# Loads in smaller pieces and a new order of the front in a spectral block with a gated feed-forward, one core

## The chip, the cores and the metric

The kernel runs on one core of one Trainium2 chip. The metric is the device time of one execution in microseconds (us). Before the change it is 486.74 us, the median of three runs (485.81 to 487.13). Five engines work side by side, each through its own queue in order: TensorE (PE, matmuls), VectorE (DVE), ScalarE (ACT), GpSimd (POOL) and SyncE (SP, which only issues DMA transfers here). They meet through semaphores.

## The reference

A is a spectral filter over one 2048 x 576 matrix, B a gated feed-forward part. Both are fed by a layer norm and added to their input. In bf16:

```python
def _A_ref(x, w_r, w_i):
    B, S, D = x.shape                       # 1, 2048, 576
    X = jnp.fft.rfft2(x.astype(jnp.float32), axes=(-2, -1))
    X = X * (w_r + 1j * w_i)                # 2048 x 289
    return jnp.fft.irfft2(X, s=(S, D), axes=(-2, -1)).astype(jnp.bfloat16)

def _B_ref(x, w_gate, w_up, w_down):        # 576 x 4608, 576 x 4608, 4608 x 576
    return (_gelu(x @ w_gate) * (x @ w_up)) @ w_down

h = x + _A_ref(_layernorm(x, axis=-1), A_w_r, A_w_i)
h2 = h + _B_ref(_layernorm(h, axis=-1), B_w_gate, B_w_up, B_w_down)
```

## The kernel before

The 2048 tokens lie in 16 tiles of 128 (tile c holds the tokens p * 16 + c). The Fourier transforms are matmuls with tables of cosines and sines that lie in device memory. The work has four parts:

- **The front** (0 to about 20 us): loads, the first layer norm, and the 128-point transforms over tokens within each tile.
- **Stages D, B, T, V, R** (to about 43 us): the transform over the 576 features (D), the 16-point transform (B, with the table BT), the product with the spectral weights (T), and the way back over 16 points (V and R, with the table VT).
- **The way back** over features and tiles (to about 55 us), with the first residual and the second layer norm.
- **The feed-forward part** (from 55 us), four blocks of 512 tokens, nearly all on TensorE.

The class `Prog` collects operations with the keys that they read and write. An operation waits for the last writer of what it reads, and for the writers and readers of what it overwrites. Each engine runs its operations in the order in which the program names them; so order is set by the order of calls, and for the front this is a string of tokens, `SEQ1`. The letter is the kind, the number the tile, the group or the output, and a last letter A, D or P names the engine:

- `B`, `b`: batch-norm statistics of one half of a tile on DVE (L496). `S`, `Q`: sum and sum of squares of a tile on ACT instead (L488, L492); `m`: square of the mean for such a tile on POOL (L499). The tiles with a `Q` are `ACT_TILES`.
- `v`: variances of a group of tiles on DVE (L505, L508). `q`: square root on ACT (L512). `c`: reciprocal on DVE (L517). The groups are tiles 0-1, 2-3, 4-6, 7-9, 10-12 and 13-15.
- `n`: the negated columns of a group's tiles on POOL (L569); `t`: copies of their tail columns on POOL (L574).
- `x`: the token table `ATB` scaled by the reciprocal deviations into `ATS` (L522 on POOL, one operation for a group; L527 on DVE, one for each tile).
- `M`: the 128-point transform of a group on TensorE (L553): five outputs in the order k = 1, 0, 3, 2, 4, each in a PSUM bank of its own. Two matmuls are needed for each tile and output, 20 for a group of two tiles and 30 for a group of three. Output n = 5 * group + place goes to bank (n + 1) mod 8.
- `k`: matmuls of zeros as fillers on TensorE (L538); the last two digits are how many.
- `E`: eviction of output n from PSUM into the tile `U` (L564). If there is an `F` with the same number, `E` takes only the first half (the frequencies that stage D takes first) and `F` the second.

`LORD` is the order of the loads of tokens (`x`, by tiles) and of the token table (`a`, by tiles), all issued by SP. Behind them SP issues the feature table FT, the first half of BT, the planes w_i and w_r of the spectral weights with VT between them, and at the end the second pieces of VT and BT. The weights are copied once more across the partitions (`dup_w`): on POOL (L732), on DVE (L730) and by DMAs from POOL's queue. The second of DVE's copies and of POOL's must be there before T2, the first of stage T.

`SEQF` is the order of the stages behind the front. It begins with D2 D0 d2 D1 d0 d1 B2 (a capital D is the first half of a product's matmuls, the small d the second half and the eviction, L642 and L608). Its banks are handed out in a fixed way: D2 writes banks 0 and 1, D0 2 and 3, D1 4 and 5, B2 6 and 7. Banks 0 and 1 held the outputs 23 and 24 of the front, so D2 waits until these are evicted. `ACT_TILES` also set how many operations compute the negative means at L747 on POOL, one for each run of tiles of a kind.

Of the kernel before, what the change touches and what calls it, by code (L numbers as in the profile page):

```python
# [20 lines left out]
NPRE = 8  # L21
PARTS = ((0, 256), (256, 512))
GROUPS = ((0, 2), (2, 4), (4, 7), (7, 10), (10, 13), (13, 16))
SEQ1 = """B0 b0 S3 B2 Q3 n0 B1 b1 b2 n1 t0 m3P t2 v0 v1 n2 t1 q0 c0 k14 x0D q1 M0 E0A S4 m4P c1 x1D n3 E2A k104 b5 t3 b7 Q4 E1A M1 E7A B5 B6 E8A b6 B7 v2 q2 B11 E5A B8 c2 x2P E3A E9A b8 b9 B9 v3 E6A n4 B12 Q13 E4A k206 M2 b10 q3 c3 b11 S13 x3P E11A B10 t4 b12 v4 E10A B14 m13P E14A M3 q4 c4 x4P E12A E13A t5 b14 E15A b15 B15 v5 E16A E18D E17A q5 M4 E20A E19A E23A c5 x5D n5 E24A F24D F23D E21A M5 E25A E26D E22A E28D E27A E29D F25A F29D F26A F27A F28A F22A""".split()
LORD = "x0-2 x2-4 a0-4 x4-8 a4-8 x8-12 x12-16 a8-16".split()
SPLIT = tuple(int(w[1:-1]) for w in SEQ1 if w[0] == "F")
ACT_TILES = tuple(int(w[1:]) for w in SEQ1 if w[0] == "Q")
SEQF = """D2 D0 d2 D1 d0 d1 B2 D5 B0 d5 T2 D3 B1 d3 D4 T0 T1 B5 d4 D8 B3 d8 D7 T3 B4 d7 V0 D6 v0 V1 T5 d6 v1 R0 V2 r0 v2 T4 B6 D9 B8 T6 V3 d9 D11 v3 d11 B7 D10 B9 d10 V6 V4 T7 v6 v4 V5 B10 v5 R1 D12 T8 r1 d12 B11 T9 V7 D14 v7 T10 d14 D13 B12 d13 D15 T11 V9 T12 d15 v9 V8 B13 v8 R2 r2 T13 B14 T14 B15 V12 V10 v12 v10 V13 V11 T15 v13 V14 v11 v14 V15 R3 v15 r3""".split()
# [9 lines left out]
def _np_bf16(a):  # L38
    npdt = mybir.dt.np(BF16)
    return np.ascontiguousarray(np.asarray(a, dtype=np.float32).astype(npdt))  # L40
# [291 lines left out]
def _build(nc, A_x, A_w_r, A_w_i, B_w_gate, B_w_up, B_w_down, out):  # L332
    P = Prog(nc)
    T = build_tables()
    dram = {n: nc.inline_tensor(_np_bf16(T[n]), name="c_" + n.lower()) for n in T}
    PE, DVE, ACT, SP, POOL = "pe", "dve", "act", "sp", "pool"
# [52 lines left out]
    BT = sb.alloc("BT", [128, 2, 2, 128], BF16)  # L389
    VT = sb.alloc("VT", [128, 6, 2, 128], BF16)  # L390
# [47 lines left out]
    def x_load(i, c0, c1):  # L438
        P.dma(SP, XO[:, c0:c1, 0:D], xv[:, c0:c1, :], f"x{i}", w=[("X", c) for c in range(c0, c1)])

    def atb_load(i, c0, c1):
        P.dma(SP, ATB[:, c0:c1, :], tabs[:, c0:c1, :], f"atb{i}", w=[("ATB", c) for c in range(c0, c1)])

    for i, w in enumerate(LORD):
        (x_load if w[0] == "x" else atb_load)(i, int(w[1:].split("-")[0]), int(w.split("-")[1]))
    P.dma(SP, FT[:, :, :].rearrange("p a b -> p (a b)"), dram["FTAB"][:, :], "ft", w=["FT"])
    P.dma(SP, BT[:, 0, :, :].rearrange("p b c -> p (b c)"), dram["BTAB"][:, 0:256], "bt", w=["BT"])

    def w_up(pl, hf):
        g0, g1 = ((0, 9), (9, 16))[hf]  # L450
# [5 lines left out]
    def w_down(pl, hf, sls=(0, 1, 2, 3), eng=SP, sem=""):  # L456
        g0, g1 = ((1, 9), (9, 16))[hf]
        src = (A_w_r, A_w_i)[pl].tensor
        for sl in sls:
            p0 = 64 * (sl // 2) + 32  # L460
            P.dma(eng, WS[p0 + sl % 2:p0 + 32:2, sl // 2, pl, g0:g1, :], bass.AP(src, (64 + 16 * (3 - sl) + 16 - g0) * K2, [[128 * K2, 16], [-K2, g1 - g0], [1, K2]]),
                  f"w{pl}{hf}{sem}", w=[("W", hf, pl, 2 + sl)])

    def w_zero(pl):
        for jp in range(2):
            P.dma(SP, WS[64 * jp + 32:64 * jp + 64, jp, pl, 0, :], bass.AP((A_w_r, A_w_i)[pl].tensor, (64 + 32 * jp) * K2, [[128 * K2, 16], [(-16 if jp else 48) * K2, 2], [1, K2]]),
                  f"wz{pl}", w=[("W", 2, pl, jp)])

    for pl in (1, 0):
        w_up(pl, 0)  # L470
        w_down(pl, 0)
    P.dma(SP, VT[:, 0, :, :].rearrange("p b c -> p (b c)"), dram["VTAB"][:, 0:256], "vt", w=["VT"])
    for pl in (1, 0):
        w_up(pl, 1)
        w_down(pl, 1, (0, 1, 2, 3) if pl else (0, 1))
    for pl in (1, 0):
        w_zero(pl)
    P.dma(SP, VT[:, 1, :, :].rearrange("p b c -> p (b c)"), dram["VTAB"][:, 256:512], "vt1", w=["VT1"])
    P.dma(SP, BT[:, 1, :, :].rearrange("p b c -> p (b c)"), dram["BTAB"][:, 256:512], "bt1", w=["BT1"])
    GORD = list(range(1, NG)) + [0]  # L480
    wkeys = [[("W", hf, pl, h) for pl in range(2) for h in range(6 if hf < 2 else 2)] for hf in range(3)]

# [99 lines left out]
    P.op(ACT, lambda a: a.activation(SA[:, 0, 0:1], EPT[:, 0:1], ACTF.Sqrt), r=["EPT"], w=[("SA0", 0)])  # L582
    for w in SEQ1:
        a = w[1:]
# [9 lines left out]
    for t, w in enumerate(SEQF):  # L594
        k, i = w[0], w[1:].rstrip("abc")
        if k in "DBVR":
            b = min((b for b in used if b not in busy), key=lambda b: used[b])
# [4 lines left out]
        elif k in "dvr":  # L602
            b = FB[k.upper(), int(i)]
# [137 lines left out]
    c = 0  # L741
    while c < NT:
        c1 = c + 1
# [5 lines left out]
        c = c1  # L749
# [34 lines left out]
    for w in SEQF:  # L784
        i = int(w[1:].rstrip("abc"))
# [26 lines left out]
    for t, w in enumerate(SEQ):  # L812
        k, i = w[0], int(w[1:].rstrip("ADSP"))
        if k in "INu":
            b = min((b for b in range(2 * ing, 4) if b not in held), key=lambda b: last[b])
# [3 lines left out]
        elif k in "ioUEae":  # L819
            b = SLOT[{"i": "I", "o": "N", "U": "u", "E": "I", "a": "N", "e": "u"}[k], i] // 2  # L820
# [145 lines left out]
    for w in SEQ:  # L966
        a = w[1:]
# [132 lines left out]
def bass_sequential_preLN__spectral_gfnet__geglu_ffn__prompt_kernel(  # L1100
    nc, A_x, A_w_r, A_w_i, B_x, B_w_gate, B_w_up, B_w_down, out
):
    _build(nc, A_x, A_w_r, A_w_i, B_w_gate, B_w_up, B_w_down, out)
# [28 lines left out]
```

## Time and profile before

| | us |
|---|---|
| median of three runs | 486.74 |
| the profiled execution | 485.97 |
| its span, from the first to the last instruction | 484.2 |
| PE busy | 477.5 |
| DVE busy | 183.3 |
| ACT busy | 146.3 |
| POOL busy | 52.2 |
| first matmul of M5, last group of the front | 18.14 |
| first matmul of stage D | 19.91 |
| first matmul of the way back (L837) | 43.62 |
| first matmul of the feed-forward part (L946) | 55.47 |

The span is some 1.8 us shorter than the execution's time, since what lies before the first and behind the last instruction is not in it. Matmuls overlap and their ends are modelled, so a row for TensorE says more by its start, and by the steps from one start to the next, than by its length. A row of the timeline gives the start, the length from the first start to the last end, the engine, the line and the tiles that are written and read, how many instructions were merged, and in brackets the idle time ahead of them with what ended it.

### The profile page before, as it was taken

The page shows a single profiled execution, that of the slowest core. Times are in us where ns is not written, and L with a number is a line of the kernel's source. Part 1 is how long each engine was busy: PE and PEld are TensorE (multiplying, and loading weights), DVE is VectorE, ACT ScalarE, POOL GpSimd, SP SyncE. Part 2 cuts the span into 40 slices and gives each one's busy share as a digit, 9 for nine tenths or more (in the row PEclk, how much of TensorE's full clock was granted, in tenths as well). Part 3 has the DMA queues.
Part 4 walks back from the last instruction along what each step waited for, and adds up shares of the span by engine and source line. Part 5 has one row for each costly group of instructions (what it writes and reads, how often), then busy time and mean ns, then how long its engine had stood idle before and what let it go on. Part 6 is the DMA issues. An engine that isn't in the chain of part 4 may idle for free.

```text
span 484.2 us, 12895 instructions
## 1 busy us (share of the span) xinstructions
PE 477.5 (99%) x5875; PEld 304.4 (63%) x5876; DVE 183.3 (38%) x366; ACT 146.3 (30%) x295; POOL 52.2 (11%) x88
## 2 busy tenths in 40 slices
PE   8999999999999999999999999999999999999998
PEld 4877765555588744444688644444788544445884
DVE  7898755665500144333200234333101233333011
ACT  6998753434300032233100132223100133223000
POOL 6873317010120000000000000000000000000000
DMA  8865889941430001000000011000000000000000
GB/s 283 215 142 160 251 279 282 374 109 27 173 100 27 26 15 23 20 1 0 3 14 15 26 24 23 13 1 1 3 14 27 14 1 1 0 1 1 3 26 26
DMA packets 28582, 33.19 MB, mean 69 GB/s; under 512 B 12640, under 2 KB 21872, under 8 KB 28528
## 3 DMA queue, kind: packets, MB, share of 16 engines
q1 hardware_dynamic: 24864, 19.87, 14.3%
q0 software_dynamic: 3664, 12.50, 8.1%
q8 instruction: 46, 0.75, 0.7%
q14 instruction: 8, 0.07, 0.1%
HBM read 26.21 MB, written 2.36 MB: 59 GB/s over the span
## 4 chain that ended last, share of the span: by engine, by line
PE 95%; DMA 1%; DVE 1%; POOL 1%; SPq 0%; issue 0%; POOLq 0%; DVEq 0%
PE PS L946 58%; PE PS L1046 27%; PE PS L642 2%; PE PS L1058 2%; PE PS L683 2%; DMA XO<-in_A_x_dram 1%; PE PS L553 1%; PE PS L662 1%; PE PS L837 1%; PE PS L996 1%; DVE XO L860 1%; SPq L242 0%; PE PS L1013 0%; PE PS L854 0%; POOL XN L569 0%
## 5 line engine op out<-in xcount | busy, mean ns | idle before, releaser
L946 PE MATMUL PS<-HT,WG 64*128 64x512 bf16 (+1 forms) x2142 | 233.5, 373 | 0.1
L946 PEld LDWEIGHTS PS<-HT,WG 64*128 64x128 bf16 x2142 | 116.1, 94 | 104.4 <-DVE AT L955 0.2
L954 ACT ACTIVATE GL<-PS 128x512 bf16<-128x512 f32 x144 | 85.7, 596 | 281.7 <-PE PS L946 281.7
L955 DVE TENSOR_TENSOR AT<-GL,PS 128x512 bf16<-128x512 bf16 x144 | 98.8, 687 | 166.0 <-ACT GL L954 166.0
L1046 PE MATMUL PS<-WD,AT 64*128 64x288 bf16 x2160 | 133.0, 283 | 0.0
L1046 PEld LDWEIGHTS PS<-WD,AT 64*128 64x128 bf16 x2160 | 114.3, 94 | 18.7
L1033 DVE TENSOR_TENSOR OS<-PS,XO 128x288 bf16<-128x288 f32 (+2 forms) x32 | 13.2, 452 | 125.5 <-PE PS L1046 118.0
L946 PE MATMUL PS<-HT,WGX 64*128 64x512 bf16 x486 | 53.5, 376 | 0.0
L946 PEld LDWEIGHTS PS<-HT,WGX 64*128 64x128 bf16 x486 | 25.7, 94 | 26.7
L863 ACT ACTIVATE OS<-XO,NM 128x576 bf16<-128x576 bf16 x15 | 11.6, 773 | 11.4 <-DVE XO L1017 11.4
L642 PE MATMUL PS<-FT,U 64*128 64x288 bf16 x160 | 13.3, 283 | 0.0
L675 DVE TENSOR_TENSOR TP<-YS,WS 128x1024 bf16<-128x1024 bf16 x16 | 11.0, 686 | 0.4 <-PE PS L683 0.2
L564 ACT ACTIVATE U<-PS 128x384 bf16<-128x384 f32 (+2 forms) x31 | 10.5, 427 | 1.2 <-PE PS L553 1.1
L496 DVE BATCH_NORM_STATS2 ST<-XO 128x6 f32<-128x288 bf16 x26 | 10.0, 441 | 1.8 <-DMA XO<-in_A_x_dram 1.8
L242 POOL DMA_DIRECT2D WG<-in_B_w_gate_dram x9 | 6.1, 679 | 35.5 <-DMA WG<-in_B_w_gate_dram 32.1
L683 PE MATMUL PS<-VT,TP 64*128 64x128 bf16 x256 | 9.9, 217 | 0.0
L553 PE MATMUL PS<-ATS,XO 128*128 128x128 bf16 x96 | 8.2, 220 | 1.5 <-POOL ATS L522 0.8
L242 POOL DMA_DIRECT2D WD<-in_B_w_down_dram x9 | 6.7, 756 | 22.9 <-PE PS L1013 22.9
L608 ACT ACTIVATE CUS<-PS 128x576 bf16<-128x576 f32 x14 | 9.1, 656 | 0.4 <-PE PS L642 0.2
L1058 PE MATMUL PS<-WD,AT 128*128 128x448 bf16 (+1 forms) x72 | 9.0, 286 | 0.0
L538 PE MATMUL PS<-ZD 128*128 128x512 bf16 x23 | 7.5, 484 | 1.5 <-POOL ZD L431 1.5
L608 ACT ACTIVATE YS<-PS 128x576 bf16<-128x576 f32 x14 | 8.8, 653 | 0.1
(88 smaller groups left out, 231.3 us busy)
## 6 DMA issues: line engine op xcount, KB each, us to landing
WD<-in_B_w_down_dram POOLq DMA_DIRECT2D x9, 576.0 KB, 13.0
WG<-in_B_w_up_dram SPq DMA_DIRECT2D x6, 576.0 KB, 6.6
WG<-in_B_w_gate_dram POOLq DMA_DIRECT2D x6, 576.0 KB, 6.2
out_dram<-OS SPq DMA_DIRECT2D x30, 72.0 KB, 1.7
XO<-in_A_x_dram SPq DMA_DIRECT2D x3, 576.0 KB, 7.1
WGX<-in_B_w_up_dram SPq DMA_DIRECT2D x2, 576.0 KB, 4.5
WGX<-in_B_w_gate_dram POOLq DMA_DIRECT2D x2, 576.0 KB, 5.8
HT<-HN SPq DMA_TRANSPOSE x60, 2.4
```

The costliest lines, as they stand in the source:

```text
L242: fn = lambda e: e.dma_start(out_ap, in_ap)
L553: P.op(PE, lambda t, b=b, lhs=lhs, p0=p0, p1=p1, s=s, e=e, o=o, c=c: t.matmul(bank(b, p0, p1, o, o + 128), lhs, ATS[:, c, :], start=s, sto ...
L608: fn = (lambda v: v.tensor_copy(dst, src)) if eng == DVE else (lambda a: a.activation(dst, src, ACTF.Copy))
L642: return P.op(PE, lambda t: t.matmul(bank(b0 + o, 0, 128, 0, 2 * HK), U[64 * h:64 * h + 64, us, 2 * i:2 * i + 2, :, :], FT[64 * h:64 * h + ...
L683: return P.op(PE, lambda t: t.matmul(bank(b0 + o, 0, 128, 128 * c, 128 * c + 128), TP[64 * h:64 * h + 64, z, o, t_, c:256:2], VT[64 * h:64 ...
L863: P.op(ACT, lambda a, c=c, out=out: a.activation(out, XO[:, c, 0:D], ACTF.Square, bias=NM[:, c:c + 1], accum_out=SB2[:, 1, c:c + 1]), r=[( ...
L946: op = P.op(PE, lambda t, h0=h0, kt=kt, wt=wt, b=b, s=(not second and j == 0), e=(second and j == n - 1): t.matmul(bank(b, 0, 128, c0, c1) ...
L954: P.op(ACT, lambda a: a.activation(GL[:, s2, :], bank(b0), ACTF.Gelu_apprx_tanh), r=[("PS", b0)], w=[("GL", s2)])
L955: P.op(DVE, lambda v: v.tensor_tensor(AT[:, f, :], GL[:, s2, :], bank(b0 + 1), op=ALU.mult), r=[("GL", s2), ("PS", b0 + 1)], w=[("AT", f)])
L1033: P.op(DVE, lambda v: v.tensor_tensor(OS[:, p % 2, d0:d1], bank(b, 0, 128, 0, d1 - d0), XO[:, c, d0:d1], op=ALU.add), r=[("PS", b), ("X", ...
L1046: e[h] = P.op(PE, lambda t, f=f, h=h, r0=r0, j=j: t.matmul(bank(b0 + h, 0, 128, 0, 288), AT[r0:r0 + 64, f, 128 * p:128 * p + 128], WD[r0:r ...
L1058: P.op(PE, lambda t, b=b, d0=d0, d1=d1, f=f, j=j: t.matmul(bank(b, 0, 128, 0, d1 - d0), AT[:, f, 128 * p:128 * p + 128], WD[:, f, d0:d1], ...
```

## The change

- The tokens of tiles 4 to 7 come as 4-5 and 6-7, and 8 to 11 as 8-9 and 10-11, with the second piece of the token table between these two.
- BT (both halves) and the first two parts of VT come as one transfer each, where their first halves were issued; the two transfers at the end fall away.
- `SEQ1` is another string. The tiles whose statistics ACT takes are 3, 5 and 8 (before 3, 4 and 13). The scalings of groups 0 and 1 are on POOL (before on DVE). The fillers are 14 and 6 (before 14, 4 and 6). The split outputs are 23, 24, 27, 28 and 29 (before 22 to 29), and the halves at the end are on other engines and in another order.

```diff
-SEQ1 = """B0 b0 S3 B2 Q3 n0 B1 b1 b2 n1 t0 m3P t2 v0 v1 n2 t1 q0 c0 k14 x0D q1 M0 E0A S4 m4P c1 x1D n3 E2A k104 b5 t3 b7 Q4 E1A M1 E7A B5 B6 E8A b6 B7 v2 q2 B11 E5A B8 c2 x2P E3A E9A b8 b9 B9 v3 E6A n4 B12 Q13 E4A k206 M2 b10 q3 c3 b11 S13 x3P E11A B10 t4 b12 v4 E10A B14 m13P E14A M3 q4 c4 x4P E12A E13A t5 b14 E15A b15 B15 v5 E16A E18D E17A q5 M4 E20A E19A E23A c5 x5D n5 E24A F24D F23D E21A M5 E25A E26D E22A E28D E27A E29D F25A F29D F26A F27A F28A F22A""".split()
-LORD = "x0-2 x2-4 a0-4 x4-8 a4-8 x8-12 x12-16 a8-16".split()
+SEQ1 = """b0 b1 B0 B1 v0 t0 b2 n1 n0 S3 q0 c0 m3P Q3 x0P B2 k14 M0 S5 v1 t1 b4 Q5 E2A B4 q1 n2 B6 E0A b7 E1A b6 m5P t3 c1 S8 v2 q2 x1P B7 t2 B9 b9 Q8 c2 E4A m8P k106 M1 B10 v3 x2P b11 E3A E6A q3 E8A b10 E5A E7A M2 c3 n3 b12 B12 B11 E10A x3P v4 b15 E9A E11A b14 q4 c4 B13 E12A b13 E14A n4 M3 E13A B15 B14 v5 E15D E16A x4P E18A t4 E17A n5 t5 q5 c5 E19A M4 E21A E22A x5D E20A E24A M5 E25A E26A E27A E28A E29A F27A E23D F29A F23A F24D F28A""".split()
+LORD = "x0-2 x2-4 a0-4 x4-6 x6-8 x8-10 a4-8 x10-12 x12-16 a8-16".split()
...
-    P.dma(SP, BT[:, 0, :, :].rearrange("p b c -> p (b c)"), dram["BTAB"][:, 0:256], "bt", w=["BT"])
+    P.dma(SP, BT[:, :, :, :].rearrange("p a b c -> p (a b c)"), dram["BTAB"][:, :], "bt", w=["BT", "BT1"])
...
-    P.dma(SP, VT[:, 0, :, :].rearrange("p b c -> p (b c)"), dram["VTAB"][:, 0:256], "vt", w=["VT"])
+    P.dma(SP, VT[:, 0:2, :, :].rearrange("p a b c -> p (a b c)"), dram["VTAB"][:, 0:512], "vt", w=["VT", "VT1"])
...
-    P.dma(SP, VT[:, 1, :, :].rearrange("p b c -> p (b c)"), dram["VTAB"][:, 256:512], "vt1", w=["VT1"])
-    P.dma(SP, BT[:, 1, :, :].rearrange("p b c -> p (b c)"), dram["BTAB"][:, 256:512], "bt1", w=["BT1"])
```

## The prediction

> **What bounds the kernel now.** I read the page first: TensorE is busy 99% of the span, and the chain that ended last lies on it for 95%. So the change can move the time only where TensorE still waits for something else, and its orders end at about 20 us. The second view is therefore the chain in order of time, cut to the first 56 us (start, length, what):
>
> ```profile
> 3.06 7.08 DMA XO<-in_A_x_dram
> ...
> 10.22 0.84 POOL XN L569
> ...
> 11.65 0.83 POOL ATS L522
> ...
> 14.53 1.85 PE PS L553 x30
> 16.38 0.09 issue
> 16.47 3.51 PE PS L553 x60
> 19.98 2.01 PE PS L642 x30
> 21.99 0.25 PE PS L662 x4
> ```
>
> Up to 14.5 us the end is set by the landing of tiles 8 to 11 (10.1 us) and then by POOL, op behind op. From 14.53 the chain is on TensorE, and in this view it stays there piece behind piece until 43.06. **So the one number that matters is when the first L642 matmul (D2, the first of stage D) can start**: 19.91 in the trace; every us of delay there is handed on to 43 us and, behind it, to the feed-forward part, which is all TensorE. Third view, POOL's queue in order of time:
>
> ```profile
> 7.72 0.35 POOL L574 TENSOR_SCALAR XN<-XO 128x192 bf16<-128x192 bf16 x1 [1.76 <-DMA XO<-in_A_x_dram]
> ...
> 11.65 0.83 POOL L522 TENSOR_TENSOR ATS<-ATB,RS 128x384 bf16<-128x384 bf16 x1 [0.17 <-POOL XN L574]
> 12.64 0.83 POOL L569 TENSOR_SCALAR XN<-XO 128x768 bf16<-128x768 bf16 x1 [0.16 <-POOL ATS L522]
> ...
> 15.50 0.83 POOL L522 TENSOR_TENSOR ATS<-ATB,RS 128x384 bf16<-128x384 bf16 x1
> ```
>
> POOL has about 0.16 us between dependent ops and 0.09 otherwise. Fourth view, the groups by line with shapes kept apart (last two numbers of a row: busy us in all, mean ns of one):
>
> ```profile
> L569 POOL TENSOR_SCALAR XN<-XO 128x512 bf16<-128x512 bf16 x2 | 1.2, 621 | 0.5 <-DMA XO<-in_A_x_dram 0.3 <-POOL XN L569 0.2
> L499 POOL TENSOR_SCALAR TM<-SA 128x1 f32<-128x1 f32 x3 | 0.8, 262 | 0.5 <-POOL XN L574 0.3 <-ACT JNK L492 0.2
> L564 ACT ACTIVATE U<-PS 128x192 bf16<-128x192 f32 x10 | 2.6, 372 | 0.1
> ```
>
> Fifth view, the end of the front on ACT and DVE:
>
> ```profile
> 19.79 1.06 ACT L564 ACTIVATE U<-PS 128x192 bf16<-128x192 f32 x4
> ...
> 18.98 1.78 DVE L564 CAST U<-PS 128x192 bf16<-128x192 f32 x5
> 20.80 0.64 DVE L730 COPY WS<-WS 64x1444 bf16<-64x1444 bf16 x1
> ```
>
> A half eviction on ACT lasts 0.37 to 0.43 us, but the next starts 0.21 later ((1.06 - 0.43) / 3).
>
> **Part 1, the loads.** Landings before, from the tile's issues taken one by one: tiles 0-1 at 3.7 us, 2-3 at 4.4, first table piece 5.7, tiles 4-7 at 7.65, second table piece 8.4, tiles 8-11 at 10.1, 12-15 at 11.5, last table piece 12.4. The bytes stay the same, two more transfers are issued. Two-tile pieces have a row (tiles 2-3 came 0.7 us behind 0-1), so I put 4-5 at 6.6, 6-7 at 7.65, 8-9 at 8.5, the second table piece at 9.2 (needed about 11), 10-11 at 10.1. Bounds for 6-7: 7.4 (two steps of 0.7 with a little loss) to 8.3 (two steps of 1.3, the first table piece's step). I take 7.65, since the same 576 KB landed then. The Trainium skill, "DMA: Bandwidth & Descriptors", section "Bandwidth", speaks against it: move 1 MiB or more at once, as each transfer has a fixed cost of about 2 us (its "Anatomy of one DMA"). The trace does not agree that this is paid per piece in a filled queue (0.7 us from piece to piece); paid in series, tiles 6-7 would be 2 us later and the sum 2 us higher.
>
> On SP two more issues are 2 x 0.47 = 0.94 us for everything behind: FT (landed 14.1, needed 19.9), BT (14.4, needed 22.0), the spectral weights. The tightest is the last piece of plane w_r, first half: issued 13.11, landed 6.7 us later at 19.84, read by DVE's copy L730 at 20.80. It moves to 20.1 (only BT's extra 64 KB at some 280 GB/s ahead of it) or to 20.8 (the issue's whole delay); its cover is 0.96 us and the later D2 of part 4 adds to it, so 0. Without cover T2, and then TensorE, would slip by what is missing. The merged BT and VT loads take two issues away at 25.06 and 25.68 (0.58 + 0.43), so SP is free at 26.1 as before, ahead of its VR copies at 29.2; their tables only land earlier. 0.
>
> **Part 2, front order on POOL.** Scaling of groups 0 and 1 moves from DVE to POOL. No row has that op on two tiles; bounds 0.55 (two thirds of 0.83) and 0.83; I take 0.6, near the negation row of the same 621 ns scale. Group 0 (x0P) ends near 6.95, M0 starts at 7.0 (7.08 before): 0. Then n2 needs tile 6: start 7.7. From there POOL's queue, op and gap, is full: n2 0.83, m5 0.43, t3 0.47, x1P 0.76, t2 0.44, m8 0.43, x2P 0.98, n3 0.99, x3P 1.00, n4 0.99, x4P 1.00: 8.3 us, so x4P ends at 16.0 (16.32 before). DVE does not hold it up: 26 statistics at 0.36 us pitch, as before, and four scalings fewer give the inputs of x2P, x3P, x4P some 1.0 to 1.4 us ahead of their turn. The ACT tiles are 3, 5, 8 in place of 3, 4, 13, three as before; the means at L747 become seven POOL ops for six, 0.3 us, hidden in POOL's idle 1.77 us before 27.89.
>
> **Part 3, TensorE's groups.** M1 at 10.2, M2 at 12.1, M3 at 14.05, M4 at 16.05 and M5 behind it (30 matmuls, 1.67 us) at 17.7, against 18.14: **-0.43 us**. Fillers go from 24 to 20 (14 + 6 for 14 + 4 + 6); all lie in waits.
>
> **Part 4, evictions at the end.** Stage D's first product writes banks 0 and 1, which hold M4's outputs 23 and 24 until both halves are out. Before, F24 and F23 went on DVE ahead of M5's own evictions. Now F23 is on ACT, behind E28, E29, F27 and F29. E29 waits for M5's last matmul (its records end 1.84 us after M5's start) and TensorE's next work, D2, waits for F23: 1.84 + 0.04 + 3 x 0.21 + 0.39 + 0.06 = 2.96 us from M5's start to D2. Before it was 19.91 - 18.14 = 1.77. **+1.2 us**, in which TensorE stands still; queued behind F23 on ACT is F28, whose bank D1 wants 0.9 us after D2 starts, in time. Bounds: +1.0 (no handover times) to +1.4 (full 0.43 us each for the last two).
>
> **Sum.** -0.43 + 1.2 = +0.77, D2 at 20.7. The downstream chain shifts as a whole. Profiled time before 485.97 (span 484.2 and 1.8 around it) gives 486.75; that execution lay 0.77 below the median of the runs, 486.74, so the time I predict for runs is **487.5**.
>
> **The rivals.**
> 1. *The pieces and POOL are dearer.* Tiles 6-7 at 8.3 (+0.6) and x1P at 0.83 (+0.24) go one for one into POOL's full queue: +1.6, **488.4**. For it: POOL has no slack behind n2, and DMA engines are full from 6 us on. Against it: the 0.7 us step.
> 2. *The matmul clock falls in the front.* The first 128x512 fillers run at 0.43 us each and later ones at 0.21, so the clock does rise with work. Between 8.1 and 12.1 us TensorE now has only 6 fillers and M1, 2.4 of 4 us; before, the fillers right ahead of M2 kept it at 2.5 of 3.4. If M2 ran at half speed (3.34 for 1.67) M5 would start 1.0 later: +1.8, **488.5**. It decides only if M2's pitch doubles from 0.056 us. The skill's "TensorE: Matmul & The Clock Gate", Part 1, has such a gate, with a free-running 3.4 us window and half speed after an idle one; no stretch of this trace shows a drop.
> 3. *Not slower: the bank wait is not there.* If D2 could start as M5 ends, only -0.43 is left, **486.3**. It decides where F23 ends before M5 does, that is 1.2 us earlier on ACT. For it: bank and queue order are read from the code, no row shows this wait. Against: ACT serves in order, and E29 cannot run before M5's end.
>
> **How the numbers follow.** Chances: forecast 0.45, rival 1 0.27, rival 2 0.13, rival 3 0.15. The range 486.4 to 489.0 leaves out half of rival 3 and the far ends of 1 and 2; the forecast's own range is 487.0 to 488.1 (part 4's bounds, and +-0.3 on M5's start). 0.3% is 1.46 us, about what a measurement of this kernel can tell from no change. Over +1.46: 0.22 of rival 1, 0.13 of 2 and 0.07 of the forecast (its terms at their upper ends), 0.42. Under -1.46: only where rival 3 meets a gain that no row shows, 0.07. Within: 0.51.
>
> **What would show it.** A TensorE gap of about 1.2 us between the last L553 and the first L642, ended by ACT's L564; M5 at 17.7; POOL without gaps over 0.2 us from 7.7 to 17.8; tiles 6-7 landed at 7.65; L553's pitch 0.056 throughout. I am wrong if D2 follows M5 at once, if POOL waits behind 7.7, or if the stretch from D2 to 43 us (23.15 us before) changes its length.

## The result and the profile after

Over 18 runs of each kernel the median went from 486.25 to 487.11 us; the ratio is 1.0016, with a 95% interval of 1.0009 to 1.0023. That is 0.78 us more by the ratio (0.86 by the medians), where 0.77 was predicted: clear of zero, and about half of the 0.3% that the prediction took as about what can be told from no change. The time itself, 487.11, is 0.4 under the predicted 487.5, since the prediction started from three runs with a median of 486.74, while all 18 have one of 486.25.

The profiled execution of the changed kernel took 488.19 us (span 486.4), the longest of its 18 runs. So its trace shows the predicted loss and something more. First the chain of the changed kernel around the end of the front, in order of time (start, length, what; its lines have numbers 2 lower than before, so L551 is the front's matmul, L562 the eviction into U and L640 stage D):

```profile
15.93 0.87 ACT U L562 x2
16.80 0.18 ACT RS L510
16.99 3.93 ACT U L562 x13
20.92 0.14 issue
21.05 2.01 PE PS L640 x30
23.07 0.27 PE PS L660 x4
```

Before, this stretch of the chain lay on TensorE from 14.53 us on, but for 0.09 us. Now it is ACT's queue of evictions up to 20.92, and TensorE follows it. Of this queue only the end costs time: E29, the eviction of M5's last output, starts at 19.91, 0.04 behind the end of M5's last matmul, and F27, F29 and F23 come behind it in steps of some 0.21 us. F23 runs from 20.55 to 20.91. The timeline of TensorE in the changed kernel shows the hole itself:

```profile
19.37 0.50 PE L551 MATMUL PS<-ATS,XN 128*128 128x128 bf16 x6
21.05 2.01 PE L640 MATMUL PS<-FT,U 64*128 64x288 bf16 x30 [1.18 <-ACT U L562]
```

1.18 us idle, ended by ACT's eviction: the bank wait. POOL's queue in the same kernel is as full as was worked out:

```profile
7.92 0.83 POOL L567 TENSOR_SCALAR XN<-XO 128x768 bf16<-128x768 bf16 x1 [0.50 <-DMA XO<-in_A_x_dram]
...
9.84 0.61 POOL L520 TENSOR_TENSOR ATS<-ATB,RS 128x256 bf16<-128x256 bf16 x1
...
11.50 0.83 POOL L520 TENSOR_TENSOR ATS<-ATB,RS 128x384 bf16<-128x384 bf16 x1 [0.17 <-POOL TM L497]
...
15.39 0.83 POOL L520 TENSOR_TENSOR ATS<-ATB,RS 128x384 bf16<-128x384 bf16 x1
```

The scaling of a group of two takes 0.61 us (0.6 was taken), and from 7.92 to 18.0 no gap is over 0.18. The second place where this execution lost time was not in the prediction. The waits of TensorE between 18 and 48 us (engine, tile and line, what it waited for: us in all, times, longest), for the changed kernel,

```profile
PE PS L835 <- DMA VR<-RB: 1.3, 1, 1.3
PE PS L640 <- ACT U L562: 1.2, 1, 1.2
PE PS L835 <- DVE V L606: 0.4, 1, 0.4
```

and for the kernel before:

```profile
PE PS L837 <- DVE V L608: 0.4, 1, 0.4
PE PS L837 <- issue: 0.3, 1, 0.3
```

The way back (L837 before, L835 after) starts with sixteen matmuls on V and then reads VR, which DMAs from SP and POOL gather out of stage R. In this execution TensorE waited 1.3 us for the last of them to land. SP's queue tells why it came so late; before, and then after the change:

```profile
36.13 0.33 SPq L242 DMA_DIRECT2D VT<-c_vtab  x1
...
37.94 4.63 SPq L242 DMA_DIRECT2D VR<-RB  x6
```

```profile
38.06 0.33 SPq L242 DMA_DIRECT2D VT<-c_vtab  x1
...
39.86 4.09 SPq L242 DMA_DIRECT2D VR<-RB  x6
```

SP holds the four tables of the way back (VT's last part, DT, IT, EYE) until the last copy of the spectral weights has landed, and six VR copies stand behind the tables. All of it is 1.93 us later, while stage D was only 1.14 later. The whole difference of the spans can be put together from single instructions of the two traces: D2 starts 1.14 later (19.91 to 21.05), the stretch from D2 to the last matmul of stages V and R is 0.13 longer, and the one from there to the first matmul on VR is 0.94 longer (2.08 to 3.02). That is 2.21 of 2.21 us (484.18 to 486.39). From the first matmul on VR to the end both take the same, 439.08 us.

### The profile page after: what moved, and what is told of

Its sections match the earlier page's. It is cut to its first block, busy times and chain, and to the rows that moved or that the text cites. A ratio compares the mean times of both kernels' runs of the same rounds, so it can differ in the third digit from the quotient of the medians.

```text
span 486.4 us, 12887 instructions
## 1 busy us (share of the span) xinstructions
PE 476.2 (98%) x5872; PEld 303.1 (62%) x5872; DVE 182.8 (38%) x358; ACT 147.1 (30%) x296; POOL 54.2 (11%) x91
## 4 chain that ended last, share of the span: by engine, by line
PE 92%; ACT 3%; DMA 2%; DVE 1%; issue 1%; SPq 0%; POOL 0%; POOLq 0%; DVEq 0%
PE PS L944 58%; PE PS L1044 27%; PE PS L1056 2%; PE PS L640 2%; ACT U L562 1%; DMA XO<-in_A_x_dram 1%; DMA VR<-RB 1%; ACT YS L606 1%; PE PS L681 1%; PE PS L994 1%; DVE XO L858 1%; PE PS L660 1%; ACT CUS L606 0%; SPq L242 0%; PE PS L835 0%
## 5 line engine op out<-in xcount | busy, mean ns | idle before, releaser
L640 PE MATMUL PS<-FT,U 64*128 64x288 bf16 x160 | 13.3, 283 | 1.2 <-ACT U L562 1.2
L562 ACT ACTIVATE U<-PS 128x384 bf16<-128x384 f32 (+2 forms) x32 | 10.9, 430 | 0.4 <-PE PS L551 0.2
L551 PE MATMUL PS<-ATS,XO 128*128 128x128 bf16 x96 | 8.2, 219 | 2.9 <-POOL ATS L520 2.6
L551 PEld LDWEIGHTS PS<-ATS,XO 128*128 128x128 bf16 x96 | 6.9, 98 | 4.3 <-POOL ATS L520 3.7
L640 PEld LDWEIGHTS PS<-FT,U 64*128 64x128 bf16 x160 | 6.9, 94 | 3.5 <-issue 1.3
```

The lines of the kernel that those rows point to most:

```text
L551: P.op(PE, lambda t, b=b, lhs=lhs, p0=p0, p1=p1, s=s, e=e, o=o, c=c: t.matmul(bank(b, p0, p1, o, o + 128), lhs, ATS[:, c, :], start=s, sto ...
L562: fn = (lambda v: v.tensor_copy(dst, src)) if eng == DVE else (lambda a: a.activation(dst, src, ACTF.Copy))
L640: return P.op(PE, lambda t: t.matmul(bank(b0 + o, 0, 128, 0, 2 * HK), U[64 * h:64 * h + 64, us, 2 * i:2 * i + 2, :, :], FT[64 * h:64 * h + ...
```

## The experiments

Each ratio is to runs of the kernel before on the same chip in the same session, with a 95% interval. e1 to e4 ran on one chip, e5 to e8 on a second, e9 and e10 on a third, so two kernels from different groups are compared by way of their ratios. e4 has 5 runs, the others have 11 or 12. Three marks of each kernel's one profiled execution go with it, as starts from its trace: M5, D2 and the time from the last matmul of stages V and R to the first on VR.

| kernel | ratio, interval | M5 | D2 | D2 - M5 | last V/R to VR |
|---|---|---|---|---|---|
| before | 1 | 18.14 | 19.91 | 1.77 | 2.08 |
| changed | 1.0016, 1.0009 to 1.0023 | 18.03 | 21.05 | 3.02 | 3.02 |
| e1 | 0.9995, 0.9985 to 1.0004 | 17.76 | 19.53 | 1.77 | 3.07 |
| e2 | 1.0009, 1.0001 to 1.0018 | 18.05 | 20.67 | 2.62 | 2.02 |
| e3 | 0.9993, 0.9980 to 1.0005 | 17.99 | 19.76 | 1.77 | 1.83 |
| e4 | 1.0052, 1.0040 to 1.0064 | 19.54 | 22.56 | 3.02 | 1.81 |
| e5 | 1.0009, 1.0000 to 1.0018 | 17.75 | 20.77 | 3.02 | 1.82 |
| e6 | 0.9983, 0.9974 to 0.9992 | 17.97 | 19.74 | 1.77 | 1.81 |
| e7 | 0.9991, 0.9979 to 1.0002 | 18.02 | 19.79 | 1.77 | 1.81 |
| e8 | 0.9990, 0.9979 to 1.0001 | 17.51 | 19.28 | 1.77 | 2.93 |
| e9 | 0.9975, 0.9964 to 0.9986 | 17.35 | 19.12 | 1.77 | 1.99 |
| e10 | 0.9989, 0.9977 to 1.0001 | 18.45 | 20.22 | 1.77 | 1.81 |

**e1: the bank wait taken out of the changed kernel.**

```diff
-... x5D E20A E24A M5 E25A E26A E27A E28A E29A F27A E23D F29A F23A F24D F28A
+... x5D E23D F23D E20A E24A M5 E25A E26A E27A E28A E29A F27A F29A F24D F28A
```

> The changed kernel with one thing altered: the second half of output 23 is evicted by DVE right behind its first half, ahead of M5, and no longer by ACT behind M5's evictions. Theory (stage D stands still for bank 0): the gap between the last L551 and the first L640 matmul falls from about 1.2 us to at most 0.1, the first L640 follows M5's start by 1.8 us in place of 3.0, and the time is 1.1 to 1.2 us under the changed kernel's, about 0.3 to 0.4 under the kernel before (0.9992 of it). Rival (the loss comes from the smaller pieces and from POOL's longer queue, the gap is covered later): the gap goes but the time stays within 0.3 us of the changed kernel's, 1.0016 of the kernel before.

The gap is gone; TensorE goes from the front's last matmuls straight to stage D (timeline of e1):

```profile
19.10 0.50 PE L551 MATMUL PS<-ATS,XN 128*128 128x128 bf16 x6
19.53 2.31 PE L640 MATMUL PS<-FT,U 64*128 64x288 bf16 x30
```

The ratio falls from 1.0016 to 0.9995, by 0.0021 or 1.0 us, near the 1.1 to 1.2 expected. Against the kernel before, e1 is not told apart from no change: in its profiled execution D2 is 0.38 earlier than there, and VR's landing takes 0.99 back (3.07 for 2.08):

```profile
45.80 0.34 PE L835 MATMUL PS<-DT,VR 64*128 64x288 bf16 x2 [1.31 <-DMA VR<-RB]
```

The rival, that the gap is covered later, falls.

**e2: the bank wait alone, put into the kernel before.**

```diff
-... E24A F24D F23D E21A M5 ... F26A F27A F28A F22A
+... E24A F24D E21A M5 ... F26A F27A F23A F28A F22A
```

> The kernel before with the one suspected step alone: the second half of output 23 moves from DVE ahead of M5 to ACT, as the fifth eviction behind M5's fourth output. Theory: ACT starts it at about 20.2 us and ends it at 20.6, so the first L642 matmul starts at about 20.65 in place of 19.9 with a gap ahead of it that the kernel before does not have, and the time is 0.7 to 0.8 us over the kernel before (1.0016). Rival (the gap does not matter, since DVE's copies L730 end only at 22.1 in the kernel before): within 0.2 us of the kernel before.

The timeline of e2:

```profile
20.67 2.01 PE L642 MATMUL PS<-FT,U 64*128 64x288 bf16 x30 [0.78 <-ACT U L564]
```

D2 starts at 20.67 where 20.65 was expected, with the wait on ACT ahead of it. The kernel is slower beyond its interval, by 0.0009 or 0.44 us; the 0.76 us of D2 lies within the interval. The rival's 0.2 us lies in it too, so the times alone don't refute it; in the two traces 0.70 of the 0.76 us reach the end (spans of 484.18 and 484.87). One eviction moved behind M5 on another engine makes a loss in a kernel that had none.

**e3 and e4: the change in two halves.** e3 has the changed loads and `SEQ1` as it was, e4 the changed `SEQ1` and the loads as they were.

```diff
-SEQ1 = """b0 b1 B0 B1 v0 t0 b2 n1 n0 S3 ... F27A E23D F29A F23A F24D F28A""".split()
+SEQ1 = """B0 b0 S3 B2 Q3 n0 B1 b1 b2 n1 ... F29D F26A F27A F28A F22A""".split()
```

This is e3 against the changed kernel; e4 is the reverse of it in the kernel before.

> The changed loads (pieces of two tiles, second table piece behind tile 9, BT and VT as one transfer each) with the front order of the kernel before. Theory (pieces cost nothing, issue delay on SP is covered): tiles 8 and 9 land near 8.5 in place of 10.1 us, POOL's negation of group 3 starts up to 0.35 us earlier, M5 with it, and the time is between the kernel before and 0.4 us under it (0.9992 to 1.0000). Rival (pieces are dearer, or SP's 0.94 us reach the spectral weights): 0.5 us or more over it (1.0010 or more), with DVE's copies L728 or T2 waiting for a landing.

> The changed front order with the loads of the kernel before. Theory: POOL's tail copy of group 3 needs tile 9, which lands at 10.1 us in place of 8.5, so x1P starts near 10.6 in place of 9.8 and POOL's full queue behind it is some 0.8 us later; with the bank wait unchanged the time is 0.8 us over the changed kernel's, 1.6 over the kernel before (1.0033). Rival (POOL's queue is not what sets M5): within 0.3 us of the changed kernel's (1.0016).

The loads alone cost nothing (0.9993; the interval, 0.9980 to 1.0005, holds 1 and excludes the rival's 1.0010, so the rival falls). In e3's trace tiles 8 and 9 landed at 7.9 us and D2 started at 19.76, 0.15 earlier. The order alone is much dearer than expected, 1.0052 in place of 1.0033. Two rows of POOL's queue in e4 tell where:

```profile
8.41 0.83 POOL L569 TENSOR_SCALAR XN<-XO 128x768 bf16<-128x768 bf16 x1 [0.95 <-DMA XO<-in_A_x_dram]
...
10.84 0.35 POOL L574 TENSOR_SCALAR XN<-XO 128x192 bf16<-128x192 bf16 x1 [1.16 <-DMA XO<-in_A_x_dram]
```

The mechanism is the expected one, the tail copy of group 3 waits 1.16 us for tile 9. But in this execution tiles 4-7 and 8-11 landed at 8.3 and 10.8, some 0.65 later than in the kernel before, whose first loads are the same (e2 and e10, with these loads too: 7.7 and 9.7, 8.0 and 10.5). Why they did is open. M5 is 1.4 us later than in the kernel before, and the bank wait adds its 3.02 - 1.77 = 1.25. So the new order needs the small pieces. With them M5 starts at 17.75 to 18.03 in four traces (changed, e1, e5, e6); with the old order it starts at 17.99 to 18.45 in five (before, e2, e3, e7, e10).

**e5, e6, e7 and e10: the second gate.** The wait of SP for the last copy of the weights is taken out; the tables then go out as soon as SP gets to them.

```diff
     def tab_load():
-        P.op(SP, None, after=[last])
         P.dma(SP, VT[:, 2:6, :, :].rearrange("p a b c -> p (a b c)"), dram["VTAB"][:, 512:1536], "vt2", w=["VT2"])
```

e5 is the changed kernel with this edit, e6 is e1 with it, e7 is e3 with it, e10 is the kernel before with it.

> The changed kernel without SP's wait for the last copy of the spectral weights ahead of the four tables of the way back (VT's last part, DT, IT, EYE), so these are issued as soon as SP has issued the first three VR copies. Theory (a second gate, behind the bank wait: later weights hold the tables, the tables hold SP's last VR copies, and the first matmul that reads VR waits for their landing): the time from the last stage V or R matmul to the first matmul on VR falls from 3.0 us to 1.8 to 2.1, SP issues the third block's VR copies as soon as their source is evicted, and the time falls by 0.3 to 0.9 us (0.9998 to 1.0011 of the kernel before). Rival (the 3.0 us are an accident of the profiled execution): the median stays within 0.2 us of the changed kernel's (1.0016). Second rival (the wait keeps the tables out of the copies' way): copies land later, stage T waits and the time rises.

> Both cures in one: F23 on DVE ahead of M5, and no wait of SP for the last weights' copy. Theory of two gates: the first stage D matmul near 19.5 us, 1.8 to 2.1 us from the last stage V or R matmul to the first one on VR, and a time 0.6 to 1.0 us under the kernel before (0.9980 to 0.9988). Rival (one gate only): as with F23 alone, 0.9995.

> The changed loads with the order of the kernel before, and without SP's wait for the last weights' copy. In that kernel the time from the last stage V or R matmul to the first on VR is already 1.8 us, so by the theory of two gates nothing is left to gain: within 0.2 us of the same kernel with the wait (0.9993, so 0.9989 to 0.9997). Rival (the tables' early issue is a gain or a loss by itself): 0.4 us or more to either side.

> The kernel before without SP's wait for the last weights' copy, nothing else. In its profiled execution 2.08 us lie between the last stage V or R matmul and the first on VR, 0.27 over the 1.81 that six matmuls and the handover leave. Theory: 0.1 to 0.4 us faster than the kernel before (0.9992 to 0.9998). Rival (the wait costs the kernel before as much as the changed one, 1 us): 0.9980 or less. Second rival (the tables get in the copies' way): slower.

In all four the time to the first matmul on VR is 1.81 or 1.82 us, which is what the eviction of V, the handover and the sixteen matmuls on V between them need (sixteen, not the six of e10's expectation). In e5's list of waits the VR landing is gone and the bank wait is left:

```profile
PE PS L640 <- ACT U L562: 1.2, 1, 1.2
PE PS L834 <- DVE V L606: 0.4, 1, 0.4
```

e6, with both gates open, is faster than the kernel before (0.9983), and 0.0012 or 0.6 us under e1, though these two intervals overlap. In e5 the ratio falls by 0.0007 against the changed kernel's, 0.3 us, and the intervals overlap; the gain lies at the lower end of what was expected and is not told apart from the rival's 0.2. e10 came out at 0.9989, with an interval that reaches from 0.9977 past 1, e7 at 0.9991 against e3's 0.9993. So in the traces the gate is there, and without SP's wait it is open. In the times only e6 lies beyond its interval, and that against the kernel before. Whether the gate costs the changed kernel more than the kernel before in most executions is not settled: there is one trace of each, and by the ratios e10 gains no less (0.0011) than e5 (0.0007).

When the gate costs time can be read from the seven kernels that keep the wait. The tables go out 15.9 us (e4), 16.2 (before, e3), 16.5 (e2), 16.9 (e1), 17.0 (changed) and 17.2 us (e8) behind the start of D2. In the first four of these the time from V and R to VR is 1.81 to 2.08 us, in the last three 2.93 to 3.07. The changed loads alone don't make the tables late. In e3, which has them and the wait, SP issues the first table a little earlier than in the kernel before (36.13):

```profile
35.92 0.33 SPq L242 DMA_DIRECT2D VT<-c_vtab  x1
```

**e8 and e9: POOL's queue.** The scaling of group 1 goes back to DVE, in e8 on top of e1, in e9 on top of e6.

```diff
-... t3 c1 S8 v2 q2 x1P B7 t2 ...
+... t3 c1 x1D S8 v2 q2 B7 t2 ...
```

> The changed kernel with F23 on DVE ahead of M5 and the scaling of group 1 back on DVE. Theory (POOL's queue is full from n2 to x4P and sets M5): x1P's 0.61 us and its gaps, some 0.7 us, leave POOL's queue, so M2 to M5 start 0.4 to 0.7 us earlier than with F23 alone (M5 at 17.1 to 17.4 in place of 17.76) and the time falls by as much, unless the later gate on VR keeps it (then 0 to 0.3). Rival (DVE is as full as POOL): its two scalings, 0.17 us each, delay the statistics and M5 stays at 17.7.

> All three cures: F23 on DVE ahead of M5, group 1's scaling on DVE, and no wait of SP for the last weights' copy. Theory (the front sets stage D's start, the VR landing is the one later gate): first stage D matmul near 19.3 us, 1.8 us from the last stage V or R matmul to the first on VR, and 0.4 to 0.5 us less than with F23 and the wait alone cured (0.9983), so 0.9972 to 0.9976 of the kernel before. Rival (stage T's copies of the weights or another landing comes next): D2 is early but the stretch from D2 to the last V or R matmul, 23.2 us, grows by as much, and the ratio stays at 0.9983.

In e8 M5 starts 0.25 us earlier than in e1, less than the 0.4 to 0.7 expected. POOL has a gap now:

```profile
10.97 0.83 POOL L520 TENSOR_TENSOR ATS<-ATB,RS 128x384 bf16<-128x384 bf16 x1 [0.73 <-DVE RS L515]
```

It waits 0.73 us for DVE's reciprocal of group 2. So POOL set M5 up to there; then DVE's reciprocal is next. The same move brings M5 0.62 us earlier in e9 than in e6, with a wait of 0.48 us at that place. How much of the expected gain is left is therefore open between 0.25 and 0.62: e1 and e6, whose fronts are the same, differ by 0.21 themselves. In time e8 is not told apart from e1 (0.9990 and 0.9995). e9 has all three cures and the lowest ratio, 0.9975 (0.9964 to 0.9986), within the expected 0.9972 to 0.9976; its interval overlaps e6's. That is about 1.2 us under the kernel before and about 2 under the changed one, by the ratios of each. From the last V or R matmul to VR e9 takes 1.99 us where 1.8 was expected, though SP no longer waits. The profile names no releaser for the 0.23 us of idle time there; the last VR copy, from POOL's queue, landed at 44.01, 0.34 before that matmul, so it may be a landing again.

## Why the prediction was right, and where not

- **What bounds the kernel.** Right. In every kernel here the stretch from D2 to the last V or R matmul is 23.03 to 23.27 us, and from the first matmul on VR to the end it is 439.1 us, but for e4's trace (1 us longer, not explained). What did not hold is that the chain behind D2 shifts as a whole: in the profiled executions D2 moves by 1.14 us and the end by 2.2, because of the landing of VR.
- **The loads at no cost.** Right as a sum, for pieces and merged tables together (e3). Tiles 6-7 landed at 7.79 where 7.65 was put, 8-9 at 8.52 where 8.5 was. The last piece of the first half of w_r landed at 19.25, even earlier than before (19.84).
- **SP's 0.94 us behind the loads, put at no cost.** This step was incomplete. I followed it to the first half of the weights, the tightest by DVE's copy, and took SP to be free in time for the VR copies. The second half of the weights leads, through POOL's last copies, to the tables on SP, and these stand ahead of the VR copies. In the profiled execution that path was 1.93 us later and cost 0.94 beyond D2's delay; by the ratios the wait costs some 0.6 us in e1 (against e6), within the intervals. That the 0.94 us of issues made the path late is not shown: in e1, e3 and e8, which have the same loads and the wait, the last copy landed at 36.39, 35.90 and 36.43 us, against 36.11 in the kernel before and 38.04 in the changed one. Why it was so late there is open.
- **POOL's queue and M5.** The mechanism was right: the full stretch from n2 to x4P lasts 8.30 us (7.92 to 16.22), 8.3 was worked out. Two terms put its end too early. POOL waited until 7.92 for tiles 6-7, so n2 did not start at 7.7 (a wait behind 7.7 was one of the named signs of being wrong). And M4 was put 0.05 us behind the end of x4P, where the kernel before shows 0.15 (16.32 to 16.47); so 0.1 of the 0.43 us of gain was not there by the prediction's own rows. The profiled executions show a gain of 0.11. The four traces of the new front named above have M5 at 17.88 in the mean, and the three of the old front with the old loads (before, e2, e10) at 18.21; as each front moves by 0.3 to 0.4 us from trace to trace, the size is not settled more closely.
- **The bank wait.** Right in place and size: 2.96 us from M5 to D2 was predicted, 3.02 measured in all three kernels that have it (changed, e4, e5). e1 and e2 take it out and put it in.
- **The sum.** 0.77 predicted and 0.78 measured. It is partly luck: in the profiled execution M5's gain was smaller than put and the VR gate, not in the sum, added 0.94, so that the span grew by 2.2. The interval of the measured time, 1.0009 to 1.0023, also holds anything from 0.4 to 1.1 us. e5's D2, at 20.77, is the closest to the predicted 20.7.
- **The rivals.** Dearer pieces: refuted by e3, by the landing of tiles 6-7 (7.14 to 7.79 in the eight traces with small pieces, where the rival had 8.3) and by x1P's 0.61. A slower matmul clock: L551's starts are 0.056 us apart throughout the front in the changed kernel too. No bank wait: refuted by e1.

## What to carry to other kernels

When an order is written anew, check not only when data are ready but who still reads the buffer that the next stage overwrites: here one eviction of 0.4 us, queued behind three others on ACT, stopped TensorE for 1.2 us, and moving it to an idle engine gave that back. A delay on a queue that "is covered" has to be followed through every transfer behind it, to the end, and not only to the nearest reader; here the path through POOL's copies and SP's tables to VR was missed. When the gain of one cure does not show (e1 against the kernel before), look for the next gate and open both: e6 shows it.

## What the runs showed of the hardware

- Evictions of 192 columns on ACT start 0.21 us apart, while one takes 0.33 to 0.43 us from start to end (the end of the front in the kernel before and the changed one): a queue of them is cheap in throughput, and the last one's reader still waits for the whole of it.
- The same first loads landed up to 1.2 us apart (tiles 12-15 at 11.1 us in e2, 11.5 in the kernel before, 11.9 in e10, 12.4 in e4), so a front that waits for landings moves from run to run: M5 starts at 18.05, 18.14 and 18.45 in e2, before and e10, whose fronts are the same up to there.
- Single DMA issues on SP now and then took 1.2 to 2.3 us in place of 0.6, without a wait (the sixth piece of w_i's second half took 1.45 us to issue in the kernel before). What these are is open.
